# Gated mix of linear attention and a GEGLU block on one core: transfers of weights and h blocks issued at other steps, weights of the last up chain in free x slots, key sums split behind the grams

## The chip, the core and the metric

The kernel runs on one core of a Trainium2 chip. The time is device time in microseconds (us). TensorE (PE) multiplies matrices into eight PSUM banks and loads its weights beside that (PEld); VectorE (DVE), ScalarE (ACT) and GpSimd (POOL) do the elementwise work; SyncE (SP) and ACT issue the transfers between HBM and SBUF. Each engine executes its own instructions in order, so an instruction that waits holds all that stand behind it on its engine.

## The reference

The output mixes two branches of the same x (2048 rows, 576 columns), all in float32.

```python
g = _sigmoid((x * gate_w).sum(-1, keepdims=True))
# branch a: linear attention, 32 heads of 18, then wo
phi = lambda t: jnp.where(t > 0, t + 1, jnp.exp(t)) + 1e-6
pq, pk = phi(q), phi(k)
kv = jnp.einsum("bhsd,bhse->bhde", pk, v)
z = jnp.einsum("bhsd->bhd", pk)
num = jnp.einsum("bhqd,bhde->bhqe", pq, kv)
den = jnp.einsum("bhqd,bhd->bhq", pq, z)[..., None] + 1e-6
a = (num / den) merged over heads @ wo
# branch b: GEGLU, 4608 hidden columns
h = _gelu(x @ w_gate) * (x @ w_up)
b = h @ w_down
return g * a + (1 - g) * b
```

## The kernel before

Each float32 operand of a product is split into a high part (rounded to the type that TensorE multiplies, by ACT) and a low part (the difference, by DVE or POOL), and a product is high by high plus high by low plus low by high. The products of branch b are made from seven block products instead of eight (the names S, T, A and B with digits are the sums and blocks that this scheme needs). The engines' order is the order of the code: nothing is rescheduled. The kernel has these stages.

1. **Keys and gate logits** (lines 166 to 410). For each of 16 row blocks `t`, `proj_mm` multiplies, `k_post` makes phi(k), `k_split` makes `pkh` (ACT) and `pkl` (DVE) and adds phi(k) to the sum `psum_k` (POOL, line 216); `grams` multiplies x by phi(k). Beside it `Early` makes the first gate and up weights (column block 0) and stores them to the DRAM buffers `wp_d`.
2. **States** (lines 420 to 495). `grams_out` splits the grams, `key_sums_split` splits `psum_k` (ACT line 458, DVE line 459), `wv_make` splits wv on ACT and POOL; `states` and `key_sums_mm` multiply.
3. **Queries and mixing** (lines 568 to 808, and 921 to 935). For four column blocks `b` of x: `query`, `den`, then `reciprocal` and `reciprocals_load` (the reciprocals of the denominators go to DRAM `rden_d` and come back broadcast over rows into `rb`), then for four pieces `t`: `scaled` (DVE lines 662 and 69, ACT line 68) and `mixed` (TensorE line 681, ACT line 686, and a store of `ga` by ACT). Block 1 is the last. Beside it x sums (`ahead`) and the weight sums of the second up block (`up_load`, `up_sums`, `up_store`) pass through three buffers `xu`.
4. **Gate and up chains** (lines 811 to 1060). `CHAINS` lists 72 chains `(p, n, m)`: half `p` of the rows, column block `n` of 256 hidden columns, `m` gate or up. A chain is seven steps of seven matmuls of 512 columns (line 826), in the order s1, s6, s7, s5, s2, s4, s3 (numbered 0 to 6). Half 0 of x lies in `xo`, half 1 in `xo2`. The weights of a gate chain lie in `W[0]` (`wg`), those of an up chain in `W[1]` (`wu`). An up chain ends with seven blocks of h stored by SP to `h_d`. Column block 0 of half 1 comes last, so the last four chains are (0,17,up), (1,17,up), (1,0,gate), (1,0,up): below they are called LAST-3 to LAST. The weights of block 0 are loaded again from `wp_d` for them, by the helper `w_load`. From LAST-3 on half 0 of x is not needed any more, and `xo` takes down weights (`wd`) and split h blocks (`hb`).
5. **Down product** (lines 1061 to 1132). 84 units of 36 matmuls of 288 columns (line 1094), each in two halves of 18; `h_load` brings the raw block of a later unit, `h_make` splits it (ACT line 999, DVE line 1000), `d_make` and `d_sum` prepare the down weights (ACT line 979, POOL lines 981 and 986), `acc_load` brings branch a (already times g), and DVE line 1102 adds the products to it.

The transfers carry eight completion semaphores in turn: a transfer is issued only when the one eight places before it in the program has landed.

Of the kernel before, what the change touches and what calls it, by code (L numbers as in the profile page):

```python
# [38 lines left out]
def tile_gated_mix(ctx, tc, xt, xs, xn, wk, wv, wq, wo, wgu, wdn, cst, out):  # L39
    nc = tc.nc  # L40
# [170 lines left out]
    def k_split(t):  # L211
        r = r_k.pop(t)
        ph, pl = pk[t] = [kp.tile([128, D], F32R, name=n) for n in ("pkh", "pkl")]
        nc.scalar.activation(ph, r, AF.Copy, bias=EPS)
        nc.vector.scalar_tensor_tensor(pl, r, EPS, f32(ph), op0=OP.add, op1=OP.subtract)
        nc.gpsimd.tensor_tensor(psum_k, psum_k, r, OP.add)
# [263 lines left out]
    rs = key_sums_split()  # L480
    for kt in range(3, 5):
        grams_out(kt)
    st, st4 = pair(), bank()
# [228 lines left out]
    up_load(1)  # L712
    up_load(2)
# [6 lines left out]
    up_sums(0)  # L720
    token_load(1)
# [6 lines left out]
    up_store(0)  # L728
# [5 lines left out]
    up_sums(2)  # L734
    up_store(1)
# [80 lines left out]
    X, ES = {0: xo}, {0: es}  # L816

    def product(p, k, m, ps, start):
        a, b = PRODUCTS[k]
        xa, wb = X[p][:, a], W[m][:, b]  # L820
        ops = []
        for kt in range(2):
            ops += [(wb[:, kt], xa[:, kt]), (wb[:, kt], xa[:, 3 + kt]), (wb[:, 3 + kt], xa[:, kt])]
        ops.append((wb[:96, 2], xa[:96, 2]))
        for i, (w_, x_) in enumerate(ops):
            nc.tensor.matmul(ps, w_, x_, start=start and i == 0, stop=i == 6,  # L826
                             skip_group_check=not start)
# [15 lines left out]
    def w_load(m, queue):  # L843
        queue.dma_start(f32(W[m]), wp_d[m])

    def gu_steps(p, n, m, first=False):

        ps, es = {}, ES[p]
# [18 lines left out]
        def s1():  # L867
            ps["a"] = bank()
            product(p, 1, m, ps["a"], True)
            nc.scalar.activation(p1, ps["a"], AF.Copy)  # L870

        def s6():
            b = bank()
            product(p, 6, m, b, True)
            nc.vector.tensor_tensor(u2, b, p1, OP.add)  # L875

        def s2():
            a = ps["a"]
            product(p, 2, m, a, False)
            if m == GATE:  # L880
                nc.scalar.activation(es[0], a, AF.Gelu_apprx_tanh)
            else:
                up(0, a)
                keep_block(A11, es[0])

        def s7():
            c = bank()
            product(p, 7, m, c, True)
            nc.vector.tensor_tensor(u3, c, u2, OP.add)  # L889

        def s5():
            d = ps["d"] = bank()
            product(p, 5, m, d, True)
            block(3, p1, d, u3)
            if m == UP:
                keep_block(A22, es[3])

        def s4():
            e = bank()
            product(p, 4, m, e, True)  # L900
# [9 lines left out]
        def s3():  # L910
            d = ps["d"]
            product(p, 3, m, d, False)
# [15 lines left out]
    nc.scalar.dma_start(f32(W[1]), wp_d[1])  # L928
    first_steps[3]()
    for t in range(BT):  # L930
        if t + 1 < BT:
            scaled(1, t + 1)
        mixed(1, t)
# [21 lines left out]
    xf = xo.rearrange("p a b c -> p (a b c)")  # L955
# [5 lines left out]
    def h_view(v):  # L961
# [3 lines left out]
    hb = ([h_view(xf[:, 6912 + i * 3072:6912 + (i + 1) * 3072]) for i in range(3)] +  # L965
          [h_view(w[:, :3072]) for w in wf])
# [51 lines left out]
    for k in range(2):  # L1018
# [5 lines left out]
            (LAST, 1): lambda: d_make(0, 3), (LAST, 4): lambda: d_sum(T4)}  # L1024
    H_AT = [(LAST - 1, 1), (LAST - 1, 3), (LAST - 1, 5)]
# [4 lines left out]
    for c, chain in enumerate(CHAINS):  # L1030
        for i, step in enumerate(first_steps if c == 0 else gu_steps(*chain)):
# [14 lines left out]
            if i == 0 and c == LAST - 3:  # L1046
                w_load(0, nc.sync)
            if i == 0 and c == LAST - 1:
                w_load(1, nc.scalar)
# [7 lines left out]
            if (c, i) in H_AT:  # L1057
                j = H_AT.index((c, i))
                h_make(j)
                h_load((2, 3, 5)[j])  # L1060
# [45 lines left out]
    for u, (s, p, k) in enumerate(UNITS):  # L1106
# [4 lines left out]
        else:  # L1111
            h_make(3)
            h_load(6)
            for t in range(4, 8):
                acc_load(0, t)
# [5 lines left out]
        if u < 3:  # L1121
            d_make(0, u + 4)
# [73 lines left out]
```

## Time and profile before

| | |
|---|---|
| time, median of 3 runs | 1518.21 us (1513.51 to 1523.46) |
| profiled execution, time | 1517.68 us |
| its span, and mean granted TensorE clock | 1515.9 us, 0.998 |
| TensorE busy | 1500.4 us, 99% of the span |
| VectorE, GpSimd, ScalarE busy | 1005.8, 719.7, 546.1 us |
| chain of waits: TensorE | 84% of the span, lines 826 and 1094 together 76% |

The span is what the trace covers; the time of the same execution is 1.8 us longer. A row of a timeline is one group of instructions: start, duration, engine, line, output and inputs, how many (x), and in brackets how long the engine had been idle before it and what ended that. A row of waits has the sum, the number and the longest. A row of windows has, after the window and its length, the busy time of PE, PEld, DVE, ACT and POOL with their instruction counts, then the granted clock of TensorE as a share of full speed, the busy share of the transfer engines, and GB/s. The duration of a group of matmuls reaches to the end of its last one, so it overlaps the start of the next group by about 0.15 us.

### The profile page before, as it was taken

Reading aid. Unit: us, or ns where it says so; the run is one execution under the profiler, and the core shown is the slowest. Engines: PE = TensorE matmul, PEld = TensorE weight load, DVE = VectorE, ACT = ScalarE, POOL = GpSimd, SP = SyncE. Lnnn points to the kernel's source line nnn. Section 1 sums busy time; section 2 is a strip of 40 time slices with the busy share of each in tenths; the row PEclk is TensorE's granted clock in tenths of the full one; section 3 lists DMA queues with packets and bytes.
Section 4 is the critical chain, followed back from the end, with each engine's and each line's share of the span. In section 5 each row is a group of like instructions: output and inputs, shape, how many; then the busy total and the mean of one; then the engine's idle time right before and its main releaser. Section 6 shows DMA issues by size and latency. Waiting matters only on the chain.

```text
span 1515.9 us, 21599 instructions
## 1 busy us (share of the span) xinstructions
PE 1500.4 (99%) x8354; PEld 1322.2 (87%) x8354; DVE 1005.8 (66%) x1322; ACT 546.1 (36%) x711; POOL 719.7 (47%) x518
## 2 busy tenths in 40 slices
PE   9999999999999999999999999999999999999999
PEld 8998889877888888888888888888789999999999
DVE  7886776385666556666556666556677767777775
ACT  6554645333222332222332222332244344444431
POOL 2674532156644644644644644643337354644620
PEclk9999999999999999999999999999999999999999
DMA  7563474672332223332223332222977656565563
GB/s 248 163 204 117 163 247 161 230 257 91 139 132 95 105 104 121 139 126 98 105 102 126 139 124 98 105 100 109 344 251 265 214 167 213 168 214 177 205 202 132
DMA packets 98494, 246.36 MB, mean 163 GB/s; under 512 B 9040, under 2 KB 36328, under 8 KB 95960
## 3 DMA queue, kind: packets, MB, share of 16 engines
q1 hardware_dynamic: 95368, 233.13, 44.1%
q10 hardware_dynamic: 3024, 11.86, 2.2%
q8 instruction: 65, 1.06, 0.3%
q14 instruction: 37, 0.30, 0.1%
HBM read 156.72 MB, written 88.24 MB: 162 GB/s over the span
## 4 chain that ended last, share of the span: by engine, by line
PE 84%; DVE 5%; DMA 4%; issue 3%; POOL 2%; ACT 2%; SPq 0%; ACTq 0%; DVEq 0%; POOLq 0%
PE bank L826 50%; PE bank L1094 26%; PE pair L199 2%; PE kpair L244 1%; PE pair L244 1%; PE bank L433 1%; PE kpair L199 1%; DMA rb<-rden_d 1%; DMA rden_d<-rb 1%; DMA xsum_d<-xu 1%; DMA xo<-h_d 1%; DVE f L854 1%; PE pair L681 1%; POOL wv L424 1%; DMA xu<-wgu 0%
## 5 line engine op out<-in xcount | busy, mean ns | idle before, releaser
L826 PE MATMUL bank<-xo,wu 128*128 128x512 f32 x1764 | 414.9, 395 | 2.9 <-DMA wu<-wp_d 2.4
L826 PE MATMUL bank<-xo,wg 128*128 128x512 f32 x1764 | 414.5, 395 | 1.6 <-DVE e L861 1.5
L826 PEld LDWEIGHTS bank<-xo,wu 128*128 128x128 f32 x1764 | 333.5, 189 | 81.2 <-DMA wu<-wp_d 2.8
L826 PEld LDWEIGHTS bank<-xo,wg 128*128 128x128 f32 x1764 | 332.0, 189 | 80.1 <-DVE e L861 2.3
L1102 DVE SCALAR_TENSOR_TENSOR acc<-bank,gate,acc 128x288 f32<-128x288 f32 x288 | 140.6, 512 | 74.4 <-PE bank L1094 69.5
L283 POOL TENSOR_TENSOR stage<-stage 128x384 f32<-128x384 f32 x132 | 155.4, 1197 | 42.8 <-DMA stage<-wgu 40.3
L870 ACT ACTIVATE p<-bank 128x512 f32<-128x512 f32 x72 | 43.0, 597 | 332.4 <-PE bank L826 332.4
L840 POOL TENSOR_TENSOR wg<-stage,wg 128x768 fp32r<-128x768 f32 (+1 forms) x34 | 72.9, 2144 | 188.4 <-ACT wg L839 187.1
L840 POOL TENSOR_TENSOR wu<-stage,wu 128x768 fp32r<-128x768 f32 (+1 forms) x34 | 80.3, 2361 | 149.1 <-ACT wu L839 147.9
L1094 PE MATMUL bank<-xo 128*128 128x288 f32 x1044 | 141.6, 295 | 1.3 <-DVE u L864 1.3
L1094 PEld LDWEIGHTS bank<-xo 128*128 128x128 f32 x1044 | 139.5, 188 | 1.6 <-DVE u L864 1.6
L981 POOL TENSOR_TENSOR xo<-stage,xo 128x432 fp32r<-128x432 f32 x44 | 64.1, 1478 | 109.7 <-ACT xo L979 109.7
L875 DVE TENSOR_TENSOR u<-bank,p 128x512 f32<-128x512 f32 x72 | 49.5, 688 | 94.2 <-PE bank L826 88.8
L981 POOL TENSOR_TENSOR wd<-stage,wd 128x432 fp32r<-128x432 f32 x40 | 58.8, 1494 | 101.9 <-ACT wd L979 101.9
L1094 PE MATMUL bank<-wd,xo 128*128 128x288 f32 x792 | 106.5, 294 | 0.0
L1094 PEld LDWEIGHTS bank<-wd,xo 128*128 128x128 f32 x792 | 105.3, 188 | 0.0
L861 DVE TENSOR_TENSOR e<-bank,u 128x512 f32<-128x512 f32 x54 | 37.1, 691 | 75.8 <-PE bank L826 75.6
L861 DVE TENSOR_TENSOR f<-bank,u 128x512 f32<-128x512 f32 x54 | 37.3, 692 | 75.3 <-PE bank L826 73.1
L851 ACT ACTIVATE f<-f 128x512 f32<-128x512 f32 x54 | 34.2, 632 | 142.5 <-DVE f L861 142.5
L986 POOL TENSOR_TENSOR stage<-stage 128x432 f32<-128x432 f32 x48 | 76.2, 1613 | 0.0
L889 DVE TENSOR_TENSOR u<-bank,u 128x512 f32<-128x512 f32 x72 | 49.8, 692 | 35.8 <-PE bank L826 33.7
L681 PEld LDWEIGHTS pair<-kw,p 126*128 126x128 f32 (+1 forms) x480 | 66.6, 193 | 5.0 <-ACT p L68 3.1
(189 smaller groups left out, 2288.5 us busy)
## 6 DMA issues: line engine op xcount, KB each, us to landing
h_d<-sx SPq DMA_DIRECT2D x108, 256.0 KB
stage<-wgu SPq DMA_DIRECT2D x34, 768.0 KB
xo<-h_d SPq DMA_DIRECT2D x29, 768.0 KB
e<-h_d SPq DMA_DIRECT2D x28, 768.0 KB
hraw<-h_d SPq DMA_DIRECT2D x27, 768.0 KB
h_d<-e SPq DMA_DIRECT2D x72, 256.0 KB
h_d<-f SPq DMA_DIRECT2D x72, 256.0 KB
stage<-wdn SPq DMA_DIRECT2D x6, 1728.0 KB
```

The lines of the kernel that those rows point to most:

```text
L199: nc.tensor.matmul(out_t[:, :n], xa, kvw[i][:rows, r, lo:lo + n], start=(k == 0), stop=(k == 13))
L283: nc.gpsimd.tensor_tensor(o, a, b, OP.subtract)
L681: nc.tensor.matmul(y[:, i, :288], p[:R, a, g], KW[g][:R, wl, i * 288:(i + 1) * 288], start=(n == 0), stop=(n == 14))
L826: nc.tensor.matmul(ps, w_, x_, start=start and i == 0, stop=i == 6, skip_group_check=not start)
L840: nc.gpsimd.tensor_tensor(w[:, i, 3:5], src[:, :, 0:2], f32(w[:, i, 0:2]), OP.subtract)
L861: nc.vector.tensor_tensor(es[i], a, b, OP.add)
L875: nc.vector.tensor_tensor(u2, b, p1, OP.add)
L889: nc.vector.tensor_tensor(u3, c, u2, OP.add)
L981: nc.gpsimd.tensor_tensor(w[:, 1, c], src[:, c], f32(w[:, 0, c]), OP.subtract)
L986: nc.gpsimd.tensor_tensor(draw[:, o, c], draw[:, x, c], draw[:, y, c], OP.subtract)
L1094: nc.tensor.matmul(y, h[:, hl, g, t * 128:(t + 1) * 128], w[:, wl, g * 288:(g + 1) * 288], start=k in (1, 5) and n == 0, stop=n == len(ops ...
L1102: nc.vector.scalar_tensor_tensor(o, y, gate[:, 1, st:st + 1], o, op0=OP.mult, op1=OP.add)
```

## The change

- `k_split`: for t = 0 and 1 the sum into `psum_k` is made by DVE instead of POOL.
- `key_sums_split()` stands behind the last two `grams_out`, not ahead of them.
- `up_load(1)` and `up_load(2)` are spread to later places; `up_store(0)` stands behind `reciprocals(3)` and `up_sums(2)`.
- The first load of `W[1]` (2240 KB, issued by ACT) moves from behind `scaled(1, 0)` to behind `scaled(1, 2)`.
- The weights of chain LAST are loaded into a part of `xo` (`last_up`, elements 5184 to 9664 of each partition) at the start of chain LAST-2, not into `W[1]` at the start of LAST-1. `product` takes the weights as an argument.
- Since `last_up` covers them, `wd[3]` is made after unit 0 instead of in chain LAST, and the split h blocks have other places: `W[1]` serves from unit 2 on. In LAST-1 two h blocks are split, after steps 3 and 5, instead of three after steps 1, 3 and 5. The third is split inside unit 0, and the load that followed it (block 5) moves there too. Each later `d_make` of the first round stands one unit later.

```diff
@@ k_split
-        nc.gpsimd.tensor_tensor(psum_k, psum_k, r, OP.add)
+        (nc.vector if t < 2 else nc.gpsimd).tensor_tensor(psum_k, psum_k, r, OP.add)
@@
-    rs = key_sums_split()
     for kt in range(3, 5):
         grams_out(kt)
+    rs = key_sums_split()
@@
     up_load(0)
-    up_load(1)
-    up_load(2)
     nc.sync.dma_start(xop_d[:, A22], f32(x_slot(3, 1)))
...
     up_sums(0)
+    up_load(1)
     token_load(1)
...
     up_sums(1)
-    up_store(0)
+    up_load(2)
...
     up_sums(2)
+    up_store(0)
     up_store(1)
@@
+    xf = xo.rearrange("p a b c -> p (a b c)")
+    last_up = xf[:, 5184:9664].rearrange("p (a b c) -> p a b c", a=7, b=5)
...
-        ps, es = {}, ES[p]
+        ps, es, w = {}, ES[p], last_up if (p, n, m) == CHAINS[-1] else W[m]
@@
     scaled(1, 0)
-    nc.scalar.dma_start(f32(W[1]), wp_d[1])
     first_steps[3]()
     for t in range(BT):
         if t + 1 < BT:
             scaled(1, t + 1)
+        if t == 1:
+            nc.scalar.dma_start(f32(W[1]), wp_d[1])
         mixed(1, t)
@@
-    hb = ([h_view(xf[:, 6912 + i * 3072:6912 + (i + 1) * 3072]) for i in range(3)] +
-          [h_view(w[:, :3072]) for w in wf])
+    hb = [h_view(v) for v in (xf[:, 9984:13056], xf[:, 13056:16128], wf[1][:, :3072], wf[0][:, :3072], xf[:, 6912:9984])]
@@
-            (LAST, 1): lambda: d_make(0, 3), (LAST, 4): lambda: d_sum(T4)}
-    H_AT = [(LAST - 1, 1), (LAST - 1, 3), (LAST - 1, 5)]
+            (LAST, 4): lambda: d_sum(T4)}
+    H_AT = [(LAST - 1, 3), (LAST - 1, 5)]
@@
-            if i == 0 and c == LAST - 1:
-                w_load(1, nc.scalar)
+            if i == 0 and c == LAST - 2:
+                nc.scalar.dma_start(f32(last_up), wp_d[1])
@@
-                h_load((2, 3, 5)[j])
+                h_load(2 + j)
@@ units
-            h_make(3)
-            h_load(6)
-            for t in range(4, 8):
-                acc_load(0, t)
+            h_make(2)
+            h_load(5)
...
         unit(u, 1)
-        if u < 3:
-            d_make(0, u + 4)
+        if not u:
+            h_make(3)
+            h_load(6)
+            for t in range(4, 8):
+                acc_load(0, t)
+        if u < 4:
+            d_make(0, u + 3)
```

On ACT, in the mixing of block 1, stood before (`p` is a scaled piece, `ga` the mixed output, `wu` is `W[1]`):

```order
L881 ACTIVATE e_2873<-bank 128x512
L68 ACTIVATE p<-r 126x640
L928 DMA wu<-wp_d_97 128x4480
L68 ACTIVATE p<-r 126x640
L686 ACTIVATE ga<-pair,gate 128x576
L688 DMA ga_d_83<-ga 128x576
L68 ACTIVATE p<-r 126x640
```

and stands now:

```order
L880 ACTIVATE e_2873<-bank 128x512
L68 ACTIVATE p<-r 126x640 x2
L686 ACTIVATE ga<-pair,gate 128x576
L688 DMA ga_d_83<-ga 128x576
L68 ACTIVATE p<-r 126x640
L932 DMA wu<-wp_d_97 128x4480
```

The load of `wu` has moved past two scaled pieces and one output piece; the piece that it now follows is the first that needs the second half of `rb`.

On ACT, from the start of chain LAST-1 to the start of chain LAST, stood before (`p_2870` is the copy of step s1, one for each chain; the gelu results are `f`; `xo<-xo` and `xo<-e` are split h blocks, `xo<-stage` split down weights):

```order
L870 ACTIVATE p_2870<-bank 128x512
L844 DMA wu<-wp_d_97 128x4480
L999 ACTIVATE xo<-xo 128x1536
L979 ACTIVATE xo<-stage 128x864
L851 ACTIVATE f<-f 128x512
L999 ACTIVATE xo<-e_3197 128x1536
L881 ACTIVATE f<-bank 128x512
L979 ACTIVATE xo<-stage 128x864
L851 ACTIVATE f<-f 128x512
L999 ACTIVATE xo<-xo 128x1536
L851 ACTIVATE f<-f 128x512
L870 ACTIVATE p_2870<-bank 128x512
```

and stands now, from the start of chain LAST-2:

```order
L1047 DMA xo<-wp_d_97 128x4480
L977 ACTIVATE xo<-stage 128x864
L869 ACTIVATE p_2870<-bank 128x512
L977 ACTIVATE xo<-stage 128x864
L850 ACTIVATE f<-f 128x512
L997 ACTIVATE xo<-xo 128x1536
L880 ACTIVATE f<-bank 128x512
L977 ACTIVATE xo<-stage 128x864
L850 ACTIVATE f<-f 128x512
L997 ACTIVATE xo<-e_3197 128x1536
L850 ACTIVATE f<-f 128x512
L869 ACTIVATE p_2870<-bank 128x512
```

The load stands one chain earlier, ahead of the first `xo<-stage` of these rows, and of the three h blocks ahead of the last `p_2870` (the copy of step s1 of chain LAST) the third is gone; the two that are left each stand behind one more gelu.

On DVE the same stretch, chain LAST-1, stood before (lines 875, 889 and 861 read PSUM banks, line 1000 makes the low part of an h block):

```order
L875 TENSOR_TENSOR u_2871<-bank,p_2870 128x512
L1000 TENSOR_TENSOR xo<-xo 128x1536
L889 TENSOR_TENSOR u_2872<-bank,u_2871 128x512
L861 TENSOR_TENSOR f<-bank,u_2872 128x512
L1000 TENSOR_TENSOR xo<-e_3197,xo 128x1536
L861 TENSOR_TENSOR f<-bank,u_2872 128x512
L1000 TENSOR_TENSOR xo<-xo 128x1536
L861 TENSOR_TENSOR f<-bank,u_2871 128x512
```

and stands now:

```order
L874 TENSOR_TENSOR u_2871<-bank,p_2870 128x512
L888 TENSOR_TENSOR u_2872<-bank,u_2871 128x512
L860 TENSOR_TENSOR f<-bank,u_2872 128x512
L998 TENSOR_TENSOR xo<-xo 128x1536
L860 TENSOR_TENSOR f<-bank,u_2872 128x512
L998 TENSOR_TENSOR xo<-e_3197,xo 128x1536
L860 TENSOR_TENSOR f<-bank,u_2871 128x512
```

One h block less stands between the bank reads; the first now follows two more of them, the second one more.

By the semaphores in turn, the load of `last_up` has the semaphore that the first h store of chain LAST-2 carries next. So SP now issues that store only when `last_up` has landed, and the other six stores of LAST-2 and the loads of h blocks 2 and 3 stand behind it on SP. Before, the load of `W[1]` had the semaphore of the first h store of chain LAST.

23 lines of the change are left out of this document (10 added, 13 removed).

## The prediction

> **What bounds the kernel now.** I read the page first, then TensorE's list of waits.
>
> ```profile
> PE 1500.4 (99%) x8354; PEld 1322.2 (87%) x8354; DVE 1005.8 (66%) x1322; ACT 546.1 (36%) x711; POOL 719.7 (47%) x518
> ...
> PE bank L826 <- DMA wu<-wp_d: 2.4, 1, 2.4
> PE pair L681 <- ACT p L68: 2.1, 1, 2.1
> PE bank L826 <- DVE e L861: 1.5, 2, 0.8
> PE bank L1094 <- DVE u L864: 1.3, 1, 1.3
> PE pair L244 <- DVE pkl L215: 0.7, 1, 0.7
> PE bank L826 <- ACT p L870: 0.5, 1, 0.5
> PE den L573 <- DVE hl L564: 0.4, 1, 0.4
> PE pair L454 <- POOL wv L424: 0.4, 1, 0.4
> ```
>
> TensorE is busy for 1500.4 of 1515.9 us, and the change removes no matmul. So it can only win idle time of TensorE, and the idle time that it can touch is short enough to be listed: 2.4, 2.1, 1.3, 0.7, 0.5, 0.4 and 0.4 us. (The 1.5 us at line 861 stand in chains that the change leaves alone.) The waits of the other engines cost nothing as long as TensorE has work.
>
> The second reading is TensorE's timeline at the two long gaps, with the granted clock behind each of them.
>
> ```profile
> 269.16 8.47 PE L681 MATMUL pair<-kw,p 126*128 126x288 f32 x60
> 279.78 10.07 PE L681 MATMUL pair<-kw,p 126*128 126x288 f32 x60 [2.15 <-ACT p L68]
> ...
> 1082.71 11.64 PE L826 MATMUL bank<-xo,wg 128*128 128x512 f32 x49
> 1096.75 8.21 PE L826 MATMUL bank<-xo,wu 128*128 128x512 f32 x28 [2.39 <-DMA wu<-wp_d]
> 1105.43 5.19 PE L826 MATMUL bank<-xo,wu 128*128 128x512 f32 x21 [0.47 <-ACT p L870]
> 1110.46 2.55 PE L1094 MATMUL bank<-xo 128*128 128x288 f32 x18
> 1114.33 12.19 PE L1094 MATMUL bank<-xo 128*128 128x288 f32 x90 [1.32 <-DVE u L864]
> ...
> 282.00:284.00 2.00, 2.00 (x10) 2.00 (x10) 0.83 (x1) 0.09 (x1) 0.00 (x0) 0.50 0.53 203
> ...
> 1096.00:1100.00 4.00, 3.25 (x8) 2.63 (x9) 0.69 (x1) 0.63 (x1) 3.50 (x4) 0.57 0.81 298
> 1112.00:1116.00 4.00, 2.68 (x20) 2.45 (x19) 3.90 (x7) 2.21 (x4) 0.00 (x0) 1.00 0.56 210
> ```
>
> A long gap costs more than itself. The same 60 matmuls take 8.47 us ahead of the gap of 2.15 us and 10.07 us behind it, 1.60 us more, while the granted clock is 0.50. Behind the gap of 2.39 us, 28 matmuls take 8.21 us; at the pace of the chain before (11.64 us for 49) they would take 6.65, so 1.56 are lost, with the clock at 0.57. The gap of 1.32 us leaves the clock at 1.00. So the two long gaps are worth 2.15 + 1.60 = 3.75 us and 2.39 + 1.56 = 3.95 us.
>
> The Trainium skill ("TensorE: Matmul & The Clock Gate", "Why this matters for your kernels") says that gaps of TensorE have to stay under some 3 us for the clock to be kept. By that rule neither gap would have cost any clock, and the gains below would be 3.2 us smaller; the rows disagree, so I count the clock.
>
> **The change part by part.** First, the first load of `W[1]`.
>
> ```profile
> 210.47 6.90 DMA rb<-rden_d
> ...
> 266.38 11.73 DMA rb<-rden_d
> ...
> 267.86 0.33 ACTq L928 DMA_DIRECT2D wu<-wp_d  x1
> ...
> 278.13 0.83 DVE L662 SCALAR_TENSOR_TENSOR r<-r,rb 126x640 f32<-126x640 f32 x1 [5.27 <-DMA rb<-rden_d]
> ...
> 289.69 5.01 PE L826 MATMUL bank<-xo,wg 128*128 128x512 f32 x21
> ```
>
> The chain of waits shows what made the gap at 277.6 us: the second broadcast of the block 1 reciprocals took 11.73 us, against 6.90 for the same transfer at 210.47, and 1.5 us after its issue ACT had started 2240 KB for `W[1]`. DVE waits for it until 278.13, ACT splits, TensorE starts 1.65 us after DVE (279.78). Now the load stands behind the piece that needs the broadcast, so it can't run beside it. At 6.90 us the broadcast lands at 273.3 and TensorE could go on at 274.9, before it runs out of work at 277.6. The gap goes: **3.75 us** (bounds 0, if the broadcast is slow for another reason, and 3.75). What is late next is the load itself. ACT now issues it at about 275 (273.3, then 0.83 us of DVE and the split). TensorE needs it when the four pieces and the rest of the first chain are through: 269.16 + 2 x 8.47 + 5.01, about 291. That leaves 16 us, and the later load of the same size took 12.1 us in a busier stretch (1084.61 to 1096.75, below). Cost nothing; if that cover were gone, each us late is a us lost.
>
> Second, the last four chains. This is the larger part, and the less certain.
>
> ```profile
> 1073.07 0.60 ACT L870 ACTIVATE p<-bank 128x512 f32<-128x512 f32 x1 [10.66 <-PE bank L826]
> 1084.61 0.35 ACTq L844 DMA_DIRECT2D wu<-wp_d  x1
> ...
> 1079.45 1.22 SPq L857 DMA_DIRECT2D h_d<-f  x2
> ...
> 1097.29 0.69 DVE L861 TENSOR_TENSOR f<-bank,u 128x512 f32<-128x512 f32 x1 [1.93 <-DMA h_d<-f]
> 1100.35 1.49 ACT L999 ACTIVATE xo<-xo 128x1536 fp32r<-128x1536 f32 x1 [1.70 <-DMA xo<-h_d]
> 1101.87 1.76 DVE L1000 TENSOR_TENSOR xo<-xo 128x1536 fp32r<-128x1536 f32 x1 [3.88 <-ACT xo L999]
> 1104.80 0.58 ACT L870 ACTIVATE p<-bank 128x512 f32<-128x512 f32 x1
> ...
> 1113.59 0.68 DVE L864 TENSOR_TENSOR u<-bank,u 128x512 f32<-128x512 f32 x1
> ...
> 1088.00:1092.00 4.00, 4.00 (x19) 3.23 (x18) 3.44 (x3) 0.44 (x1) 3.12 (x2) 1.00 1.04 376
> ```
>
> The load now starts behind the copy at 1073.07, 11 us earlier, into slots that no matmul reads. At the same 12.1 us it lands near 1086, and TensorE wants it at 1094.3: the 3.95 us of the gap are won. But two more waits stand behind that gap, and both come from ACT and DVE being late, not from TensorE. ACT's copy of step s1 of chain LAST ends at 1105.38 because it stands behind the gelu results of LAST-1 and the third h block, which waited 1.70 us for its transfer, after DVE had waited until 1097.29 for a store of `f`. TensorE without the gap reaches s2, the first step that needs that copy, at about 1094.3 + 6.65 = 1100.9 (four steps, 28 matmuls). So the copy has to come 4.5 us earlier than it did, or the gap only moves there.
>
> Taking the third h block out brings it forward by that wait and by the split: on the old dates, DVE 1097.29 to 1097.98, gelu to 1098.6, the second h block (1.49 on ACT, 1.76 on DVE) to 1101.9, bank read to 1102.5, gelu and copy to 1103.7. That would still leave 2.8 us of wait. (Bank reads are taken at 0.7 us, like the row of 0.69, gelu results at 0.6, like the copy's 0.58.) The rest has to come from the store of `f`. Its queue changes: SP holds all seven stores of LAST-2 until `last_up` has landed (the semaphore, near 1086), where the first went out at 1079.45. Then they go out at once, 7 x 256 KB, with nothing of 2240 KB beside them. At 376 GB/s the five up to the one that DVE needs (1.3 MB) take 3.5 us, and the fifth goes out 4 x 0.61 = 2.4 us behind the first (1.22 us for two issues); done together that is 1089.5, one after the other 1092. I take 1091.5, and the bank read can't start before TensorE has done its step, at 1082.7 + 6 x 1.66 = 1092.7. Then bank read, gelu, second h block, bank read, gelu and copy (0.7 + 0.6 + 1.5 + 1.8 + 0.7 + 0.6 + 0.6 = 6.5) end near 1099, and s2 doesn't wait. If ACT's load is slowed by the stores and h loads beside it and lands at 1088, the copy ends near 1101 and s2 waits some tenths.
>
> The 1.32 us at the first down unit are the same lateness: DVE's bank reads of chain LAST begin at that copy and run without a break, to line 864 at 1113.59 to 1114.27, 8.9 us after it. With the copy at 1099 to 1101 they end at 1108 to 1110; TensorE, entering the unit near 1105.7, wants the bank 2.5 us later, at 1108.2. I leave 0.8 us of wait. Sum for this place: 3.95 + 0.47 + 1.32 - 0.8 = **4.9 us** (bounds 5.7 with no wait left; about 0 with 2.8 us at s2, 1.6 of clock behind it and the 1.32).
>
> The h blocks and down weights that moved into the down product have rows to lean on.
>
> ```profile
> 1117.32 0.92 ACT L979 ACTIVATE wd<-stage 128x864 fp32r<-128x864 f32 x1
> 1132.43 1.50 ACT L999 ACTIVATE xo<-hraw 128x1536 fp32r<-128x1536 f32 x1 [4.40 <-DMA hraw<-h_d]
> ...
> 1118.31 2.19 POOL L981 TENSOR_TENSOR wd<-stage,wd 128x432 fp32r<-128x432 f32 x2 [7.24 <-ACT wd L979]
> ```
>
> A block is split in the middle of unit u for unit u + 3. A unit takes 12.19 / 90 x 36 = 4.9 us, so there are 12.2 us, less 1.5 and 1.8 for the split: 8.9 us of slack. Here ACT waited up to 4.40 us for blocks and TensorE not at all. One more block of 768 KB behind the start of the units adds 2.1 us at 376 GB/s: 6.5 of 8.9 used, no cost. Each `d_make` of the first round has two units instead of three, 9.8 us, for 0.92 us on ACT and 2.19 on POOL: no cost. The next fetch of down weights waits for the last of them, some 5 us later than now; it is first needed two units on.
>
> Third, the start and the key sums.
>
> ```profile
> 22.14 1.43 POOL L216 TENSOR_TENSOR psum_k<-psum_k,e 128x576 f32<-128x576 f32 x1 [2.27 <-DVE gate L209]
> 22.74 1.44 DVE L215 SCALAR_TENSOR_TENSOR pkl<-e,pkh 128x576 fp32r<-128x576 f32 x1 [0.69 <-ACT pkh L214]
> 32.29 0.74 DVE L215 SCALAR_TENSOR_TENSOR pkl<-e,pkh 128x576 fp32r<-128x576 f32 x1
> ```
>
> `pkl` takes 1.44 us beside POOL's sum and 0.74 without it, and TensorE waits 0.7 us for the one of t = 1. With both sums on DVE, each behind its `pkl`, `pkl` ends 0.7 us sooner and the added sum (an estimate of 0.7 us, from the 0.74 of an operation of the same size) fills what was freed: **0.7 us** won, at worst 0.7 lost. The key sums go behind two splits that the states need first; TensorE's wait there is for POOL's `wv` (0.4), which stays. The spread weight sums let the reciprocals of block 3 pass a store on SP; TensorE's wait of 0.4 us for `hl` may go. For these two together **0.4 us** (bounds 0 and 0.8).
>
> The sum: 3.75 + 4.9 + 0.7 + 0.4 = 9.75, say 9.7 us. The profiled execution took 1517.68 us (span 1515.9), 0.5 below the median of the runs, so it stands for them: 1517.7 - 9.7 = **1508 us**, 0.6% faster.
>
> **The rivals.** (1) The gap only moves: the load lands no earlier than 1090, since the transfer engines are full at this place (busy share 1.04 at 1088 to 1092), the seven stores held on SP come after it, and the copy at s2 is late by the 2.8 us worked out above. The same bytes pass the same engines either way. The Trainium skill says so too ("DMA: Bandwidth & Descriptors", "Issuing engines are not separate DMA queues"): transfers issued by different engines interleave on the same 16 engines. The saturated row agrees. Then this place gives nothing: 1517.7 - 4.85 = 1512.8 us. Against it: `last_up` has 20 us, not 10. Chance 0.2. (2) The change doesn't do what it says at 277 us: the broadcast, 1 KB pieces, is slow for its own sake; then 1517.7 - 6.0 = 1511.7 us. For it: only one row of each kind. Against it: 6.90 beside other transfers. Chance 0.1. (3) Slower: the h blocks. All blocks from number 5 on come later behind the eight `acc` loads, TensorE runs out when they are over 8.9 - 4.4 = 4.5 us later than now, and each us beyond that is lost, with 1.6 us of clock. To end slower than before they have to be about 4.5 + 9.7 - 1.6 = 12.6 us later, 4.7 MB at 376 GB/s, where 0.8 MB were added. At 16 us later: 1508 + 11.5 + 1.6, about 1521 us. Chance 0.05.
>
> **How the numbers follow.** The forecast has 0.6, the rivals 0.2, 0.1 and 0.05; 0.05 are for what I don't see. All gains in full (3.75 + 5.7 + 0.7 + 0.8 = 10.95) give 1506.7, and the runs of the kernel before spread by 5 us to either side of their median, so the low end is 1502. The high end takes in the first two rivals with their spread: 1517. A change of 1% is about what a measurement of this kernel can tell from none, and 1% is 15 us. All gains together are 11 us, so faster by more than that needs a run spread on top: 0.07. Slower by over 1% needs 25 us of stall that the forecast lacks, which only something I don't see could bring: 0.05. The rest, 0.88, is within 1%.
>
> **What would show it.** Right: TensorE's waits lack both rows of 2.1 and 2.4 us; the granted clock stays at 1.00 at 280 and 1096 us; the broadcast takes about 7 us; `pkl` takes 0.74 us twice at the start. Wrong: a wait of line 826 for ACT's copy or for `f` of 2 us or more in chain LAST (rival 1), a wait for `wu` at the first up chain, a wait of line 681 for the split again (rival 2), or any wait of line 1094 for a split h block (rival 3). A span that falls by less than 5 us with both gaps gone would show that I mis-sized the clock.

## The result, and the profile after

The changed kernel took 1513.06 us (median of 20 runs, 1507.72 to 1515.58) beside 1516.88 us of the kernel before (20 runs, 1513.51 to 1523.46): a ratio of 0.9969, 95% interval [0.9958, 0.9979]. By the ratio that is 4.7 us less (the medians differ by 3.8), about half of the 9.7 us that the prediction added up. The profiled execution took 1515.58 us (span 1513.8), and it is the slowest of the 20.

TensorE's list of waits after the change:

```profile
PE bank L828 <- ACT p L869: 5.0, 2, 3.1
...
PE bank L828 <- DVE f L860: 0.8, 1, 0.8
```

The waits for `wu`, for the split of line 68, for `u` at the down unit and for `pkl` are gone. In their place stands one row that was 0.5 us before: TensorE waits twice for ACT's copy `p`, 5.0 us in all. (Line 826 of before is 828 now, 870 is 869, 861 is 860, 1094 is 1092.) TensorE's timeline at the two places (start, length, what, how many, the idle time ahead of it and what ended it):

```profile
269.10 16.45 PE L681 MATMUL pair<-kw,p 126*128 126x288 f32 x120
290.24 6.61 PE L828 MATMUL bank<-xo,wu 128*128 128x512 f32 x28
299.98 6.68 PE L828 MATMUL bank<-xo,wu 128*128 128x512 f32 x21 [3.13 <-ACT p L869]
...
1081.89 10.00 PE L828 MATMUL bank<-xo,wg 128*128 128x512 f32 x42
1092.65 1.89 PE L828 MATMUL bank<-xo,wg 128*128 128x512 f32 x7 [0.75 <-DVE f L860]
1094.38 6.73 PE L828 MATMUL bank<-xo,xo 128*128 128x512 f32 x28
1102.98 6.72 PE L828 MATMUL bank<-xo,xo 128*128 128x512 f32 x21 [1.88 <-ACT p L869]
1109.54 10.10 PE L1092 MATMUL bank<-xo 128*128 128x288 f32 x72
```

The 120 matmuls of block 1 now run in one piece, and the last chains don't wait for their weights. But each place has a new gap further on, at step s2 of an up chain (the first up chain, and LAST), and the 21 matmuls behind each take 6.7 us where they take 5.0 elsewhere. So the clock went down again, as the windows show (the number behind the five engines is the granted clock):

```profile
302.00:304.00 2.00, 2.00 (x6) 1.60 (x5) 1.97 (x3) 0.36 (x1) 1.92 (x2) 0.50 0.20 80
...
1104.00:1108.00 4.00, 4.00 (x13) 3.13 (x12) 2.46 (x4) 0.00 (x0) 0.26 (x1) 0.63 0.51 196
```

What led to the first new gap is read from the timelines of SP, DVE and ACT, and from the chain of waits (the last two rows: start of a transfer and us to its landing):

```profile
266.58 0.76 SPq L650 DMA_DIRECT2D rb<-rden_d  x1
273.29 0.83 DVE L662 SCALAR_TENSOR_TENSOR r<-r,rb 126x640 f32<-126x640 f32 x1 [0.49 <-DMA rb<-rden_d]
...
274.80 0.42 ACTq L932 DMA_DIRECT2D wu<-wp_d  x1
...
289.17 0.74 ACT L686 ACTIVATE ga<-pair,gate 128x576 f32<-128x576 f32 x1 [6.83 <-DMA ga_d<-ga]
292.38 1.06 ACT L1013 ACTIVATE xo<-f 128x1024 fp32r<-128x1024 f32 x1 [1.44 <-DMA ga_d<-ga]
299.35 0.58 ACT L869 ACTIVATE p<-bank 128x512 f32<-128x512 f32 x1
...
278.40 10.69 DMA ga_d<-ga
289.94 2.29 DMA ga_d<-ga
```

The broadcast landed at 273.3, as forecast, and `W[1]` came in time. But ACT could not write its last `ga` until an earlier store of `ga` had landed, 6.83 us, and then waited for one more. The earlier store, issued 3.6 us behind the 2240 KB, took 10.69 us; the one more, issued at 289.94, took 2.29. Behind these stand, in ACT's order, gelu, a split of block sums, gelu, a split, gelu and the copy `p`, with DVE's splits and bank reads in between. TensorE had reached s2 at 296.9.

And for the second gap, from the timelines of SP, DVE and ACT, and from the windows (in each, the last three numbers are the granted clock, the busy share of the transfer engines and GB/s):

```profile
1083.91 0.32 SPq L992 DMA_DIRECT2D e<-h_d  x1
1084.32 0.86 SPq L856 DMA_DIRECT2D h_d<-f  x2
...
1091.90 0.69 DVE L860 TENSOR_TENSOR f<-bank,u 128x512 f32<-128x512 f32 x1 [3.33 <-PE bank L828]
1096.34 0.68 DVE L860 TENSOR_TENSOR f<-bank,u 128x512 f32<-128x512 f32 x1
...
1102.35 0.58 ACT L869 ACTIVATE p<-bank 128x512 f32<-128x512 f32 x1
...
1084.00:1088.00 4.00, 4.00 (x19) 3.22 (x18) 3.83 (x6) 1.14 (x2) 2.78 (x2) 1.00 0.88 251
1088.00:1092.00 4.00, 3.90 (x17) 2.81 (x15) 0.67 (x2) 0.00 (x0) 0.15 (x1) 1.00 1.01 387
```

SP stood at the second h load until 1083.91 (8.3 us, for a store of `e`) and sent the stores of `f` only then. DVE's read of s5's bank, which writes into `f`, came at 1091.90; the matmuls of s5 had ended at about 1088.5 (1081.89 + 4 x 1.66). The row puts the idle time down to TensorE, but that had long been done: it was the first store, 7.6 us after its issue at 1084.32. The second h load, 768 KB, had left just ahead of it, and the transfer engines were nearly or wholly busy. From the bank read the copy is 10.5 us away.

### The profile page after: what moved, and what is told of

Read it like the earlier page. It is cut to its first block, busy times and chain, and to the rows that moved or that the text cites. A ratio compares the mean times of both kernels' runs of the same rounds, so it can differ in the third digit from the quotient of the medians.

```text
span 1513.8 us, 21594 instructions
## 1 busy us (share of the span) xinstructions
PE 1500.9 (99%) x8354; PEld 1323.3 (87%) x8354; DVE 1003.3 (66%) x1324; ACT 546.2 (36%) x711; POOL 718.7 (47%) x516
## 4 chain that ended last, share of the span: by engine, by line
PE 91%; DVE 3%; issue 2%; ACT 2%; DMA 1%; POOL 1%; SPq 0%; ACTq 0%; POOLq 0%; DVEq 0%
PE bank L828 53%; PE bank L1092 26%; PE bank L433 3%; PE pair L681 2%; PE pair L199 2%; PE kpair L244 1%; PE pair L244 1%; PE kpair L199 1%; DMA ga_d<-ga 1%; POOL wv L424 1%; PE den L573 0%; DMA raw<-wk 0%; DVE f L853 0%; ACT p L68 0%; DVE r L662 0%
## 5 line engine op out<-in xcount | busy, mean ns | idle before, releaser
L828 PE MATMUL bank<-xo,wu 128*128 128x512 f32 (+1 forms) x1715 | 403.4, 396 | 3.1 <-ACT p L869 3.1
L828 PEld LDWEIGHTS bank<-xo,wu 128*128 128x128 f32 (+1 forms) x1715 | 324.4, 189 | 79.0 <-ACT p L869 3.6
L1092 PE MATMUL bank<-wd,xo 128*128 128x288 f32 x1008 | 135.8, 294 | 0.0
L1092 PEld LDWEIGHTS bank<-wd,xo 128*128 128x128 f32 x1008 | 134.1, 188 | 0.0
L1092 PE MATMUL bank<-xo 128*128 128x288 f32 x792 | 107.1, 295 | 0.1
L1092 PEld LDWEIGHTS bank<-xo 128*128 128x128 f32 x792 | 105.7, 188 | 0.5 <-DVE u L863 0.4
L850 ACT ACTIVATE e<-e 128x512 f32<-128x512 f32 x54 | 34.1, 633 | 91.2 <-DVE e L860 90.8
```

Source lines behind the costliest of these rows:

```text
L850: nc.scalar.activation(es[i], es[i], AF.Gelu_apprx_tanh)
L1092: nc.tensor.matmul(y, h[:, hl, g, t * 128:(t + 1) * 128], w[:, wl, g * 288:(g + 1) * 288], start=k in (1, 5) and n == 0, stop=n == len(ops ...
```

## The experiments

Three sets of four kernels, each set on a chip with its own runs of the kernel before: 1518.93, 1517.8 and 1517.26 us. "The two last chains" is the time from the start of LAST-1 to the first down unit. The runs are few and their intervals overlap: only the eleventh kernel's interval lies wholly below that of the changed kernel's 20 runs. What an edit did at its place is read from its profile, one execution each.

**The changed kernel once more** (no edit).

> The changed kernel once more, for a second profile beside the other runs of this chip. Its first profiled execution (1515.58 us) was the slowest of 20 (median 1513.06), so its stalls may be its own. Theory S: the two new stalls belong to the kernel. The second profile then shows a wait for ACT's copy p near 300 us of some 3 us with the clock lost behind it (21 matmuls in 6.7 us where 5.0 is the pace), and waits for f and for p of together 2 to 3 us near 1092 and 1102 us; the time is 1511 to 1515 us, ratio to before about 0.997. Theory R (the stalls vary from run to run): one of them or both are missing or under 1 us in the second profile, and its span is shorter than 1513.8 by what is missing (4.8 us and 4.3 us).

It took 1512.85 us, ratio 0.9962 [0.9949, 0.9974], span 1510.2. Theory S holds, with one part of R. TensorE's timeline:

```profile
297.89 6.40 PE L828 MATMUL bank<-xo,wu 128*128 128x512 f32 x21 [3.01 <-ACT p L869]
...
1100.94 5.18 PE L828 MATMUL bank<-xo,xo 128*128 128x512 f32 x21 [1.88 <-ACT p L869]
```

Both gaps for `p` are there, and the one for `f` with 0.79 us, but behind the same 1.88 us the clock was kept this time (5.18 us for the 21). The span is 3.6 us shorter than in the first profile: 1.5 us of it this clock, 1.9 us the work ahead of 257 us, the same code in both.

**`W[1]` started by SP.**

```diff
     for k in range(2):
         s_load(k)
+    nc.sync.dma_start(f32(W[1]), wp_d[1])
     w_fetch(1, 0)
...
-        if t == 1:
-            nc.scalar.dma_start(f32(W[1]), wp_d[1])
```

> The changed kernel, with the first load of W[1] started by SP, behind SP's two loads of block sums, instead of by ACT between its stores of ga. Theory A (own queue): ACT waited 6.83 us at 289 us for a ga buffer because the store of ga stood behind 2240 KB in ACT's own queue; with the load in SP's queue the stores leave at once, ACT's waits of 6.83 and 1.44 us go, TensorE's wait of 3.13 us near 300 us and the 1.7 us of clock behind it go: 4.8 us faster than the changed kernel, about 1508 us, ratio to before 0.994. Rival B (transfer engines): the same bytes pass the same engines at the same time, so the ga stores land as late as before and the wait stays: 1513 us, ratio 0.997. Rival C (the broadcast): anything of 2240 KB that starts before the block 1 reciprocals are through slows them, and the gap at 277 us comes back: 1512 us, with a wait at line 681.

1511.77 us, ratio 0.9960 [0.9946, 0.9975]: by the time not to be told from the changed kernel. The timelines of SP, ACT and TensorE:

```profile
275.58 0.32 SPq L1016 DMA_DIRECT2D wu<-wp_d  x1
278.11 0.33 ACTq L688 DMA_DIRECT2D ga_d<-ga  x1
287.04 0.74 ACT L686 ACTIVATE ga<-pair,gate 128x576 f32<-128x576 f32 x1 [4.52 <-DMA ga_d<-ga]
297.85 5.12 PE L828 MATMUL bank<-xo,wu 128*128 128x512 f32 x21 [0.85 <-ACT p L869]
```

With `W[1]` in another engine's queue ACT still waits 4.52 us for its stores, so theory A falls in the main: the stores are slow because 2240 KB pass the same transfer engines, less because of the queue. Rival C falls too: no wait of line 681 came back. The Trainium skill ("DMA: Bandwidth & Descriptors", "Issuing engines are not separate DMA queues") says that transfers issued by different engines share the same 16 engines; the rows agree. The 2.3 us by which the wait is shorter were enough to cut the gap to 0.85 us and keep the clock.

**The first two h loads later.**

```diff
-            if (c, i) == (LAST - 2, 0):
+            if (c, i) == (LAST - 2, 4):
                 h_load(0)
                 h_load(1)
```

> The changed kernel, with the loads of the first two h blocks started behind the stores of A22 and A11 of chain LAST-2 (step 4 of that chain instead of step 0). Theory D (SP held): in the changed kernel SP stands at the second h load until 1083.9 us, and the stores of f stand behind it, so that DVE gets f only at 1091.9; now the first two stores leave near 1079 and 1080 us, and the load that comes next is the one that is held. DVE's bank read of step s5 of LAST-1 then starts when TensorE is done (about 1088.5 to 1089), the copy p of chain LAST comes 3 us earlier, and TensorE's waits of 0.75 and 1.88 us and the 1.7 us of clock behind them go: 4.3 us faster than the changed kernel, about 1509 us, ratio 0.9945. Rival E (transfer engines): the stores of f leave early but land no earlier, since 2240 KB and the h blocks fill the engines until 1090; the waits stay, 1513 us, ratio 0.997. Rival F: the h blocks, now later, become what ACT waits for, and the wait for p at s2 stays or grows: 1513 us or more.

1511.48 us, ratio 0.9953 [0.9934, 0.9973], short of the theory's 1509. Theory D holds for the order of events, as the timelines of SP, DVE and TensorE show:

```profile
1078.39 1.54 SPq L856 DMA_DIRECT2D h_d<-f  x2
1082.84 0.32 SPq L992 DMA_DIRECT2D xo<-h_d  x1
...
1089.31 0.69 DVE L860 TENSOR_TENSOR f<-bank,u 128x512 f32<-128x512 f32 x1
...
1100.39 5.18 PE L828 MATMUL bank<-xo,xo 128*128 128x512 f32 x21 [0.89 <-ACT p L869]
```

The stores leave 6 us sooner, DVE reads the bank without a wait, and TensorE's wait of 0.8 us for `f` is gone. The wait for `p` is halved, not gone.

The edit lifts two holds at once, which the expectation didn't say. With the h loads behind them, the first two stores no longer stand eight places behind the early load either; the first h load does now, and SP stood at it for 2.9 us, for `last_up`, until 1082.84. That is 11.2 us after the issue of that load, so in the changed kernel the early load alone would have held the first store until about 1083 (an estimate: 1072.26, its issue there, and 10 to 11 us). What each hold is worth by itself was not measured.

**`W[1]` at its old place.**

```diff
     scaled(1, 0)
+    nc.scalar.dma_start(f32(W[1]), wp_d[1])
     first_steps[3]()
...
-        if t == 1:
-            nc.scalar.dma_start(f32(W[1]), wp_d[1])
```

> The changed kernel, with the first load of W[1] back at its old place, ahead of the last step of the first four and the pieces of block 1. Theory: place 1 was given back as a whole. The gap at 277 us (2.15 us and 1.60 of clock) returns, the wait of 3.13 us and the 1.7 of clock near 300 us go: 1.1 us faster than the changed kernel, within the uncertainty of it, 1511 to 1513 us, ratio 0.996 to 0.997. Rival G (the new stall near 300 us has another cause, as the order of the up_load and up_store steps): the wait near 300 us stays and the gap at 277 us comes on top, 1516 to 1517 us, ratio 1.000.

1516.03 us, ratio 0.9975 [0.9959, 0.9992]. The wait near 300 us is gone and the old gap is back, so rival G falls; but the gap is larger than in the kernel before:

```profile
281.86 9.91 PE L681 MATMUL pair<-kw,p 126*128 126x288 f32 x60 [5.27 <-ACT p L68]
```

5.27 us and 1.44 of clock (9.91 - 8.47), against 2.15 and 1.60. So the early load cost more than the one profile of before had shown, and the theory's time (1511 to 1513 us), which took the gap at 2.15 us, is missed by 3 us.

**Two splits of block sums moved into the third chain.**

```diff
-    S_AT = [(0, 4), (0, 5), (2, 4), (2, 6), (3, 1), (3, 3)]
+    S_AT = [(2, 1), (2, 2), (2, 4), (2, 6), (3, 1), (3, 3)]
```

> The changed kernel, with the first two splits of block sums for the second half of x (ACT line 1013, DVE line 1014) moved from the last steps of the first chain to steps 1 and 2 of the third chain. W[1] is still started by ACT behind the split of piece 1. Theory H: the wait for p near 300 us is a chain on ACT and DVE, late copy of ga (held by the ga stores that share the engines and the queue with W[1]), then gelu, split, bank read, gelu, split, bank read, gelu, copy p; without the two splits in it the copy p comes near 293 us, 4 us ahead of TensorE, even though the wait for the ga store (5 to 7 us) stays. TensorE's wait of 3.0 to 3.3 us and the 1.4 to 1.7 us of clock behind it go: 4.5 us faster than the changed kernel (1512.85 on this chip), about 1508.5 us, ratio to before 0.993. Rival I: the wait for the ga stores alone delays ACT so far that the copy stays late: no gain, 1513 us. Rival J: the splits are late for the third and fourth chain instead, and a wait of line 828 for e or p of 1 us or more appears between 310 and 335 us: 1510 to 1512 us.

1512.36 us, ratio 0.9967 [0.9954, 0.9979]: no gain. The gap near 300 us is gone, though ACT still waits 6.55 us for a store, so rival I falls. But rival J is right, and at a higher price than it had. The timelines of DVE, GpSimd and TensorE:

```profile
307.43 3.35 DVE L1014 TENSOR_TENSOR xo<-f,xo 128x1024 fp32r<-128x1024 f32 x1 [0.53 <-POOL wu L843]
320.33 1.23 DVE L1014 TENSOR_TENSOR xo<-f,xo 128x1024 fp32r<-128x1024 f32 x1 [2.04 <-ACT xo L1013]
...
307.27 2.44 POOL L842 TENSOR_TENSOR wu<-stage,wu 128x1024 fp32r<-128x1024 f32 x1
...
313.65 3.35 PE L828 MATMUL bank<-xo,wg 128*128 128x512 f32 x7 [3.52 <-DVE e L860]
```

A split that takes 1.23 us elsewhere took 3.35 us beside GpSimd's splits of the next weights, and the bank read behind it came too late for s3.

**The second h split in LAST**, with the h loads at step 4 as above.

```diff
-    H_AT = [(LAST - 1, 3), (LAST - 1, 5)]
+    H_AT = [(LAST - 1, 3), (LAST, 1)]
```

> The changed kernel, with the first two h loads behind the stores of A22 and A11 as in the run before, and the split of the second h block moved from step 5 of LAST-1 to step 1 of LAST. Theory D': what was left of the wait for p at s2 (0.89 us with the loads moved alone) was that split, 1.5 us on ACT and 2.1 us on DVE, between two bank reads of LAST-1. Without it the copy p of LAST comes near 1096 us, ahead of TensorE; both waits (0.8 and 1.9 us) and the clock behind them, where it was lost (0 to 1.7 us), go: 2.7 to 4.3 us faster than the changed kernel, 1508.5 to 1510 us, ratio 0.993 to 0.994. Rival K: the split moved into LAST makes DVE late there, and the first down unit waits for a bank read of LAST (1 to 2 us) or for the fourth h block: then 1511 to 1512 us.

1510.17 us, ratio 0.9954 [0.9938, 0.9971]. Theory D' holds; in TensorE's timeline the last chains have no gap at all:

```profile
1081.33 11.64 PE L828 MATMUL bank<-xo,wg 128*128 128x512 f32 x49
1092.81 11.64 PE L828 MATMUL bank<-xo,xo 128*128 128x512 f32 x49
1104.29 10.10 PE L1092 MATMUL bank<-xo 128*128 128x288 f32 x72
```

The two last chains take 22.96 us, against 27.75 in the kernel before.

**Both edits together** (the sums as in the fifth run, the h blocks as in the sixth).

> Both edits together: the splits of block sums in the third chain, the h loads behind two stores and the second h split in LAST. If both places are independent, the gains add: 4.5 + 2.7 to 4.3 = 7 to 9 us faster than the changed kernel, 1504 to 1506 us, ratio to before 0.990 to 0.9915, which is what the forecast of 9.7 us below before would have given or a little more. If the gain at the first place is absorbed later, as by DVE in the chains behind it, the time is no better than the better one of the two, 1508 us.

1509.12 us, ratio 0.9945 [0.9930, 0.9960]. The second alternative: the gain at the first place is given back at 315 us (a wait of 3.51 us for `e`, the same as in the fifth run).

**The last up weights loaded as before.**

```diff
-            if i == 0 and c == LAST - 2:
-                nc.scalar.dma_start(f32(last_up), wp_d[1])
+            if i == 0 and c == LAST - 1:
+                nc.scalar.dma_start(f32(W[1]), wp_d[1])
...
-        ps, es, w = {}, ES[p], last_up if (p, n, m) == CHAINS[-1] else W[m]
+        ps, es, w = {}, ES[p], W[m]
```

> The changed kernel, with the weights of the last up chain loaded into W[1] behind the first step of LAST-1, as in the kernel before; the h blocks and down weights stay where the change puts them. Theory: the early load was worth the gap of 2.39 us and its 1.56 us of clock, less the waits of 0.8 and 1.9 us that took its place (and 0 to 1.7 us of clock): 0 to 1.3 us slower than the changed kernel, 1513 to 1514 us, ratio about 0.997. Rival L: the load in its old place lands no later than TensorE wants it, since the third h block no longer goes beside it, and the early load was worth nothing or less: 1510 to 1512 us. Rival M: the full forecast of 4.9 us for this place was right and the loss is elsewhere: 1517 to 1518 us.

1511.44 us, ratio 0.9957 [0.9943, 0.9972]: rival L. The timelines of SP and TensorE:

```profile
1077.77 0.32 SPq L992 DMA_DIRECT2D e<-h_d  x1
...
1101.02 5.19 PE L828 MATMUL bank<-xo,wu 128*128 128x512 f32 x21 [0.98 <-ACT p L869]
```

The second h load leaves 6 us sooner than beside the early load, the weights land in time without being early, and the two last chains take 24.21 us, against 26.16 and 27.65 in the two profiles of the changed kernel. What helped at this place is the other half of the change, the third h block and a `d_make` moved into the down product.

**The start alone**, on the kernel before: the two edits at lines 216 and 480 of the change.

> The kernel before, with only the start of the change: the two first sums psum_k on DVE and the key sums split behind the grams. The forecast counted 0.7 us for the first and up to 0.4 us for the second (with the spread of the weight sums, which is not in this kernel). Theory: the profile shows pkl in 0.74 to 0.77 us twice and no wait of TensorE for pkl of 0.7 us; the time is 0.4 to 1.1 us less than before, ratio 0.9993 to 0.9997, which the interval can't tell from 1. Rival N: the start is worth much more than its wait, since the first 257 us differ by 2 us between executions of one kernel: ratio 0.998 or less. Rival O: the DVE sums cost as much as they free: ratio 1.000, and a wait for a later pkl or kvw in the profile.

1518.3 us, ratio 1.0006 [0.9992, 1.0020]: no gain to be seen; 0.7 us is not excluded by the interval's lower end. Rival N falls; the time can't tell the theory from rival O. The profile shows `pkl` as forecast and, of itself, a second look at the gaps of before:

```profile
22.72 0.76 DVE L215 SCALAR_TENSOR_TENSOR pkl<-e,pkh 128x576 fp32r<-128x576 f32 x1 [0.69 <-ACT pkh L214]
...
281.92 10.20 PE L681 MATMUL pair<-kw,p 126*128 126x288 f32 x60 [5.19 <-ACT p L68]
...
1098.65 8.36 PE L826 MATMUL bank<-xo,wu 128*128 128x512 f32 x28 [2.13 <-DMA wu<-wp_d]
```

The wait for `pkl` is gone. The start of the first gate chain lies at 257.79 us here, at 258.71 in the kernel before, and between 255.94 and 259.13 in all other profiles: that spread covers any gain of the start.

**The block sums behind s5.** `S_AT` is [(2, 3), (2, 4), (2, 6), (3, 0), (3, 1), (3, 3)], the h blocks as in the sixth run.

> The changed kernel, with the h loads behind two stores and the second h split in LAST as in the run without waits in the last chains, and the splits of block sums in the third chain, but now behind the bank read of s5 (steps 3, 4 and 6 of the third chain, 0 and 1 of the fourth) instead of at steps 1 and 2, where DVE's splits took 3.35 and 1.68 us beside GpSimd's splits and held back the bank read that TensorE waited 3.5 us for. Theory: the gap has then no place left in these chains; the stretch from the first x7 of the first gate chain to the third up chain, 59.3 us in that run and in the changed kernel, takes 55.5 to 56.5 us, and the time is 1505.5 to 1507 us, ratio to before 0.992. Rival P: the delay goes on to the fourth chain (s2 there waits for the copy p, or the fifth chain for the split block sums): the stretch up to the third up chain is short, but the one behind it grows from 764 to 766 us or more, and the time is 1508 to 1509 us.

1508.17 us, ratio 0.9950 [0.9930, 0.9969]: rival P. The first stretch falls to 54.16 us, but the one behind it grows from 764 to 768.41. TensorE's waits:

```profile
PE bank L828 <- POOL xo L1014: 1.9, 1, 1.9
...
PE bank L828 <- ACT p L869: 1.0, 1, 1.0
```

The splits have to be made before the fifth chain, and at each of the three places tried TensorE waits, for them or for what stands behind them.

**`W[1]` on SP and the second h split in LAST.** The edits of the second, third and sixth run.

> The changed kernel, with W[1] started by SP behind the block sums (57.6 us in the first stretch, against 59.3) and with the h loads and the second h split as in the run without waits in the last chains (22.96 us for the last two chains, against 26.2 to 27.7). If the two places are independent the gains add, 1.7 to 1.8 us and 3.2 to 4.7 us: 5 to 6 us faster than the changed kernel, about 1507 to 1508 us, ratio 0.9925 to 0.9935. If not, the time is that of the second edit alone, 1510 us, 0.995.

1507.26 us (1505.23 to 1509.89), ratio 0.9935 [0.9917, 0.9952]. The gains add, this has the lowest median of the study, and the last chains again run without a gap. TensorE's timeline:

```profile
1077.78 11.64 PE L828 MATMUL bank<-xo,wg 128*128 128x512 f32 x49
1089.26 11.64 PE L828 MATMUL bank<-xo,xo 128*128 128x512 f32 x49
```

**The late load with the second h split in LAST.** The edits of the eighth run and the `H_AT` of the sixth.

> The changed kernel with the weights of the last up chain in W[1], loaded behind the first step of LAST-1 as before, and the second h split in LAST; the h loads stay at step 0 of LAST-2. It asks if the early load into the x slots is worth anything once the h blocks are out of the way. Theory Q: no. With the late load SP's second h load left at 1077.8 us instead of 1083.9, the stores of f behind it came in time, and the wait of 0.98 us left at s2 was the second h split; without it the last two chains take 22.96 to 23.5 us, and the time is 1510 us, the same as with the early load and the h loads moved (1510.17). Rival R: the load in its old place collides with the stores and lands after 1093.3 us: a wait for wu of 1 us or more in LAST, the two chains take 24.5 us or more, 1511.5 us or more.

1510.18 us, ratio 0.9956 [0.9938, 0.9973]. Between Q and R, nearer to Q: the wait for the weights is there, but short.

```profile
1094.99 11.74 PE L828 MATMUL bank<-xo,wu 128*128 128x512 f32 x49 [0.63 <-DMA wu<-wp_d]
```

The two last chains take 23.86 us, 0.9 more than with the early load and the h loads moved, and the time is the same (1510.17). So the early load is worth under 1 us once the h blocks are out of its way; where they aren't, it loses to the late load (26.16 and 27.65 against 24.21 us).

## Why the prediction was half right

The direction and the range held. The range, 15 us wide, had been drawn to take in the first two rivals. The size did not hold, and the stretches of TensorE's timeline say where it went: from the first gate chain's first step to the second up chain (the fourth chain; the tenth expectation calls it the third up chain), over the two last chains, and from the first down unit to the end of the span. Each number is the difference of the starts of two rows; the middle stretch, 764 us, is the same in all of these.

| kernel | first stretch | two last chains | from the down unit on |
|---|---|---|---|
| before | 59.92 | 27.75 | 405.44 |
| start alone on before | 63.08 | 27.48 | 405.44 |
| changed | 59.42 | 27.65 | 404.26 |
| changed, once more | 59.27 | 26.16 | 404.23 |
| `W[1]` at its old place | 62.94 | 25.72 | 404.31 |
| h loads later | 59.65 | 24.11 | 404.29 |
| second h split in LAST | 60.43 | 22.96 | 404.21 |
| last up weights as before | 60.63 | 24.21 | 404.25 |
| `W[1]` on SP, second h split in LAST | 57.85 | 22.95 | 403.77 |

- **The first load of `W[1]`, 3.75 us.** The gap went for the reason given: the broadcast took 6.7 us (266.58 to 273.29) where it had taken 11.73. Its size was a single profile's: in the two other kernels that load early it was 5.2 and 5.3 us of idle time. The step that failed is "What is late next is the load itself" with its "Cost nothing". The load was in time. Late next was ACT, which the step named only as the engine that issues it: its `ga` buffers were held by stores that share the transfer engines with the 2240 KB, and two splits of block sums stood between that and the copy `p`. The new gap cost 2.7 to 3.5 us of idle time and 1.4 to 2.9 of clock. The six executions with the load at its new place on ACT and the splits of sums unmoved average 59.8 us for the first stretch, 59.3 to 60.6, the three with the load at its old place 62.0, 59.9 to 63.1: 2.2 us won.
- **The last chains, 4.9 us.** The gaps of 2.39 and 1.32 us went. Two steps failed. The first is the landing of the held stores: released near 1086, they were to "go out at once", and 3.5 us were reckoned for five of them at 376 GB/s. They left sooner than that, from 1084.32, but the first alone took 7.6 us, beside the second h load, which that term doesn't have. The second is the date of the bank read, "the bank read can't start before TensorE has done its step", 1092.7. The store stopped not the read of s4 but the one of s5 before it (1091.90), and between the two reads stands the first h block, which the sum left out; s4's bank was read at 1096.34. From there the step's 6.5 us were right: the copy ended at 1102.93, 6.6 later. That SP would hold the stores was seen, and the early load did hold them, by the third run until about 1083. That the second h load would hold them too was not: it waited for stores of `e` that shared the engines with the early load, until 1083.91 (1077.77 with the late load). Won: 27.6 to 26.1 us (means of the two and of the five executions with this code), and 1.2 us from the down unit on, 2.7 in all.
- **The start and the key sums, 0.7 and 0.4 us.** The wait for `pkl` went; no time could be measured from it. The wait of 0.4 us for `hl` is gone in the profile of the changed kernel and is back in that of the sixth run, where the code there is the same.
- **The rivals.** Rival 1 (the gap only moves, since the stores held on SP make the copy late) is what happened at the last chains in part, with a wait of 1.88 us, and its mechanism at the first place with another store and another engine. It was given 0.2; the same question was not asked for the first place. That its time, 1512.8 us, is close to the measured 1513.06 is luck: it has the first place in full and nothing at the last chains, where 2.2 and 2.7 us were won. By the prediction's own sign for it (a wait of 2 us or more in chain LAST) the 1.88 us fall just short. Rival 2 falls with the 6.7 us (its "1 KB pieces" are rows of 5 KB: 630 KB for 126 partitions). Rival 3 falls: no unit waits for an h block.

The sum of the measured parts, 2.2 + 2.7 = 4.9 us, agrees with the 4.7 us of the ratio, as closely as averages over a few executions can. With the two new waits shortened or removed (`W[1]` on SP, second h split in LAST) the kernel took 0.9935 of the time before, 9.9 us less: the forecast amount was there, behind two further waits. It is shown that the second gap goes when the h loads and the second split are moved; the share of the h loads' own hold and of the early load's is open. For the first, it is shown that ACT's chain to `p` makes it and that the load's queue is not the main cause; with the load at its old place it is gone, but a later load, at a time without `ga` stores, was not tried.

## What to carry to other kernels

When a large load is moved, list every transfer that runs or is queued in its new place, the stores too, and follow each to the buffer it frees and the engine that needs that buffer: here the moved load was in time and the stores beside it, of 288 and 256 KB, were late. When a gap of the bottleneck engine is closed, look up what the next step needs at the earlier date, with all that its engine must do before that. Price a gap from more than one execution: the same gap was 2.15 us in one profile and over 5 in two.

## What was not expected of the hardware

- Whether a gap of TensorE costs clock is decided near 2 us here, and not always alike. Behind 1.88 us, 21 matmuls took 6.72 us in the first profile of the changed kernel and 5.18 in the second, and 5.17 to 5.20 in three more runs; behind 0.85 to 1.02 us the clock was kept every time, behind 2.13 us and more it was lost every time. The Trainium skill ("TensorE: Matmul & The Clock Gate", "Why this matters for your kernels") puts the bound at about 3 us; these rows disagree.
- A store of 288 KB took about 9 us to land beside a load of 2240 KB from another queue: with the load on SP, ACT waited until 287.04 for the store that it had issued at 278.11. With the load in the same queue it was 10.69 us, and 2.29 us for a store issued 15 us behind the load.
